# Last channel stage of an inverse 2D FFT: even classes as pairs of 64 by 64 products, joined on VectorE

## Chip, core and metric

The kernel runs on one core of a Trainium2 chip. The metric is device microseconds (us) of one execution of the kernel, as a median over runs. Engines are written as in the profile: PE is TensorE (matmuls), PEld its weight loads, DVE is VectorE, ACT is ScalarE, POOL is GpSimd, SP is SyncE, which issues most DMAs here.

## What is computed

Two branches work on the same layer norm of x (2048 tokens by 512 channels, bfloat16) and are added to x:

```
xn = _layernorm(A_x)
X  = rfft2(xn, axes=(-2, -1)) * (w_r + 1j*w_i)          # tokens and channels
A  = irfft2(X, s=(2048, 512), axes=(-2, -1))
B  = (gelu(xn @ w_gate) * (xn @ w_up)) @ w_down         # 512 -> 1792 -> 512
out = A_x + A + B
```

## The kernel before

All operations are put down in a list, each with an engine, an assumed cost, what it reads and writes, and a key. A planner (`_Sched`) simulates them and fixes one static order for each engine; a semaphore count joins engines. PE gets the spectral products as soon as the plan has their inputs ready, and the dense products of branch B as filler in all other places.

Branch B works on four blocks of 512 tokens and 14 slices of 128 hidden columns. `gated` (L718) makes four 128x512 products for gate and four for up into one of three PSUM banks each, ACT evicts them (L723 gelu into `gg`, L724 copy into `uu`, four buffers each), and DVE multiplies (L725) into `hT`. `down` (L766) sums 14 products into the bank `ps_dn`; ACT evicts it (L774 into `db`, two buffers) and DVE adds it to `x_sb` (L775). For the last block, `down` goes to `ps_sp` and DVE adds straight from PSUM (L777); these are the last 70 matmuls of the program.

Branch A is a DFT in stages. Forward over channels (L635), DVE butterflies, forward over tokens (L850, and L854 for class v=0), the filter on DVE, then the two stages that matter here:

- **Inverse token products, `f_i`.** Eight classes v; in each, for two halves kp and for even and odd channel frequencies o, one product with the real part (L931) and one with the imaginary part (L932). The spectrum X is the stationary operand, 128 channel frequencies taken with step 2, so that output partition (lane) = channel frequency. Each is a 128x128 product that streams 128 columns: eight to a class, 64 in all. ACT evicts each class from a pair of PSUM banks (L937).
- **Last channel stage, `f_b`.** After butterflies over tokens (DVE, through the helper `tt`, L467), DVE makes `zi` in `specC`. For each of eight pairs jp of token groups, eight products (L991) of 128 lanes by 128 columns: two token groups o by four classes cc (cosine even, cosine odd, sine even, sine odd frequencies; matrix `Ti`, 128 lanes x 128 positions each). ACT evicts 1024 columns (L996) into R in `specB`. DVE then adds and subtracts even and odd, cosine and sine, each time filling a mirrored half: `eo` (L467, 1024 elements, two), `y` (two), and adds `y` to `x_sb` (2048 elements). This goes on for each quarter jq, and SP stores the quarter of the output (L782).

The PSUM pairs of branch A come from a pool of two (`ps_sp`, name "sp" in the code). R, `eo` and `y` lie in `specB` (12288 elements a partition), which the token butterflies used before.

The products of the stage before the change, as the code has them:

```
for o in range(2):
    for cc in range(4):
        ins = e.matmul(spb(t, o, cc * P, P), zi.ap[:, 2 * jp + o, cc, :], Ti.ap[:, cc, :], start=(cc == 0), stop=(cc == 3))
```

One more place in the kernel matters for reading the change: L854, the v=0 class of the forward token stage. It multiplies 64 lanes by 512 columns, four times, the two halves of the lanes alternating and going to different PSUM banks:

```
for i in range(0 if v else 2):
    for r in range(2):
        l = slice(64 * r, 64 * r + 64)
        ins = e.matmul(spb(t, r), tf.ap[l, 2 * r + i], H.ap[l, hh[i]], start=(i == 0), stop=(i == 1))
```

Of the kernel before, what the change touches and what calls it, by code (L numbers as in the profile page):

```python
# [7 lines left out]
ACT = mybir.ActivationFunctionType  # L8
ALU = mybir.AluOpType
BF16 = mybir.dt.bfloat16  # L10
# [5 lines left out]
P = 128  # L16
# [21 lines left out]
def _constants():  # L38
    npbf = mybir.dt.np(BF16)
    th = 2.0 * np.pi / S  # L40
    m = np.arange(P)
    K = np.zeros((8, P))
    mm = 31 - m + 64 * (m // 32)
    K[0] = np.where(m < 64, 8 + 16 * mm, 16 * (mm - 63) * (m != 96))
    for c in range(1, 8):
        K[c] = c + 16 * mm
    q = np.arange(P) + 0.5
    ph = th * q[:, None, None] * K[None]
    co, si = np.cos(ph), np.sin(ph)
    si2 = si.copy()  # L50
    si2[:, 0, 96] = np.sin(th * q * 1024)
    cof = co.copy()
    cof[:, 0, 96] *= 0.5
    low = (m < 64)[None]
    tf = []
    for a in (cof, si2):
        for part in (1, np.where(low, -1, 1)):
            e = a[:64, 0] * part
            tf.append(np.concatenate([e, 0 * e] if a is cof else [0 * e, e]))
    for c in range(1, 8):  # L60
        r = np.sin(np.pi * c / 2)
        f = (r, r) if c % 2 else (-1.0, 1.0) if c == 4 else (1.0, -1.0)
        tf.append(np.concatenate([co[:64, c], f[0] * si[:64, c]]))
        tf.append(np.concatenate([co[:64, c], f[1] * si[:64, c]]))
    tf = np.stack(tf, 1)
    ci, sv = co[:64].transpose(2, 1, 0), si2[:64].transpose(2, 1, 0)
    sg = np.array([0, 1, 1, -1, 1, 1, 1, -1])[:, None]
    pr = np.concatenate([ci, -sg * sv], 2)
    pi = np.concatenate([sv, sg * ci], 2)
    lo = (m < 64)[:, None]  # L70
    for a in (pr, pi):
        half = a[:, 0, 0:64].copy()
        a[:, 0] = np.concatenate([half * ~lo, half * lo], 1)
    ti = np.stack([pr, pi, -pi], 2)
    a = 2.0 * np.pi / D * (np.arange(P) + 0.5)[:, None]
    ke = 2 * np.arange(P)[None]
    kse = ke.copy()
    kse[0, 0] = 256
    T = np.stack([np.cos(a * ke), np.cos(a * (ke + 1)), np.sin(a * kse), np.sin(a * (ke + 1))], 1)
    al = np.full((P, 4), 2.0)  # L80
    al[0, 0] = al[0, 2] = 1.0
    Ti = T.transpose(2, 1, 0) * al[:, :, None] / (S * D)
    fwd = []
    a = 2.0 * np.pi / D * (np.arange(P) + 0.5)[:, None]
    for r in (0, 2):
        kk = np.arange(r, 256, 4)[None]
        fwd += [np.cos(a * kk), np.sin(a * np.where(kk == 0, 256, kk))]
    odd = np.concatenate([np.arange(1, 256, 4), np.arange(3, 256, 4)])[None]
    fwd += [np.cos(a * odd), np.sin(a * odd)]
    small = np.concatenate([np.eye(P)] + fwd + [Ti.reshape(P, 512)], 1)  # L90

    def cvt(z):
        return np.ascontiguousarray(z.reshape(P, -1).astype(np.float32).astype(npbf))

    return cvt(small), cvt(tf), cvt(ti)
# [49 lines left out]
class _Sched:  # L145
# [11 lines left out]
    def op(self, eng, cost, fn, reads=(), writes=(), tiles=(), key=0.0, after=(), dma=0, lag=0.0, due=None, land=None):  # L157
        o = _Op()
        o.eng, o.fn, o.cost, o.key, o.dma, o.lag, o.due, o.land = eng, fn, cost, key, dma, lag, due, land
        o.reads, o.writes, o.tiles = reads, writes, [(t, False) for t in tiles]  # L160
        o.extra = [a for a in after if a is not None]
        o.seq = len(self.ops)
        o.end = None
        o.pos = None
        self.ops.append(o)
        return o
# [184 lines left out]
def bass_parallel_sum__spectral_gfnet__glu_gated_geglu__prompt_kernel(  # L351
# [22 lines left out]
    op = sch.op  # L374

    with ExitStack() as es:
        def sb(name, shape, dt=BF16, cell=0):
            n = int(np.prod(shape))
            t = es.enter_context(nc.sbuf_tensor(name, [P, n], dt))
            return view(t, name, 0, shape, cell)  # L380

        def view(t, name, lo, shape, cell=0):
            n = int(np.prod(shape))
            ap = t[:, lo:lo + n]
            if len(shape) > 1:
                names = "abcdef"[:len(shape)]
                ap = ap.rearrange("p (%s) -> p %s" % (" ".join(names), " ".join(names)), **dict(zip(names[1:], shape[1:])))
            return _V(ap, name, np.arange(lo, lo + n).reshape(shape), cell or (64 if n > 512 else 1))
# [8 lines left out]
        wu = sb("wu", [4, FF])  # L397
        wd = sb("wd", [NFC, D])
        small = sb("smallc", [9, P])
        tf = sb("tokf", [18, P])  # L400
        ti = sb("toki", [8, 3, P])
        W = sb("filt", [2, 2, 8, 257], cell=1)
        w1 = sb("filt1024", [2, 512])
        edge = sb("edge", [2, 8, 2])
# [10 lines left out]
        RB = region("specB", 12288)  # L415
# [7 lines left out]
        Ti = small[:, 5:9]  # L423
# [16 lines left out]
        def spb(t, h, lo=0, n=512):  # L440
            b = (2 * t.slot + h) * 512 + lo
            return ps_sp[:, b:b + n]

        def spair(t):
            return ps_sp[:, t.slot * 1024:(t.slot + 1) * 1024]
# [10 lines left out]
        def c_act(n):  # L456
            return 0.05 + n * 0.00085
# [8 lines left out]
        def tt(o, a, b, f, n, key=0.0, **kw):  # L466
            return op("dve", c_tt(n), lambda e: e.tensor_tensor(o.ap, a.ap, b.ap, f), reads=(a, b), writes=(o,), key=key, **kw)  # L467

        ADD, SUB, MUL = ALU.add, ALU.subtract, ALU.mult
# [114 lines left out]
        X = R1(0, [8, 2, D])  # L584
# [259 lines left out]
        for v, hh in ((4, (12, 13)), (0, (14, 15)), (2, (8, 9)), (6, (10, 11)), (1, (0, 1)), (7, (4, 6)), (3, (2, 7)), (5, (5, 3))):  # L844
            t = _T("sp")
# [73 lines left out]
        for i, v in enumerate((0, 4, 1, 7, 2, 6, 3, 5)):  # L919
            t = _T("sp")  # L920

            def f_i(e, v=v, t=t):
                ins = None
                xr, xi = ((0, 2), (1, 2)) if v == 0 else ((0, 3), (1, 1))
                for kp in range(2):
                    for o in range(2):
                        lo = 256 * kp + o
                        pr = X.ap[:, v, 0, lo:256 * kp + 256:2]
                        pi = X.ap[:, v, 1, lo:256 * kp + 256:2]
                        bank = spb(t, kp, 256 * o, 256).rearrange("p (x i) -> p x i", x=4)  # L930
                        e.matmul(bank[:, xr[0]:xr[0] + xr[1] + 1:xr[1]], pr, ti.ap[:, v, 0], start=(o == 0), stop=False)  # L931
                        ins = e.matmul(bank[:, xi[0]:xi[0] + xi[1] + 1:xi[1]], pi, ti.ap[:, v, 1 + kp], start=False, stop=(o == 1))  # L932
                return ins

            op("pe", 8 * 0.057, f_i, reads=(X[:, v], ti[:, v]), tiles=(t,), lag=0.1)
            gv = G[:, i].tr((1, 0, 2))
            op("act", c_act(1024), lambda e, gv=gv, t=t: e.activation(gv.ap, spair(t).rearrange("p (k x i) -> p k x i", k=4, x=4), ACT.Copy),  # L937
               writes=(gv,), tiles=(t,), key=-0.5)
# [36 lines left out]
            tt(Yb[:, h:h + 4], Yb[:, h:h + 4], od[:, h:h + 4], ADD, 2048)  # L975
        Yi = R1(0, [16, 2, 4, 64])
        zi = R3(0, [16, 4, P])
        R = RB(0, [8, 2, 4, P])
        for jq in range(4):
            js = slice(2 * jq, 2 * jq + 2)  # L980
            a = Yi[:, 4 * jq:4 * jq + 4]
            tt(zi[:, 4 * jq:4 * jq + 4, :, 64:P], a[:, :, 0], a[:, :, 1], ADD, 1024)
            tt(zi[:, 4 * jq:4 * jq + 4, :, 63::-1], a[:, :, 0], a[:, :, 1], SUB, 1024)
            for jp in (2 * jq, 2 * jq + 1):
                t = _T("sp")

                def f_b(e, jp=jp, t=t):
                    ins = None
                    for o in range(2):
                        for cc in range(4):  # L990
                            ins = e.matmul(spb(t, o, cc * P, P), zi.ap[:, 2 * jp + o, cc, :], Ti.ap[:, cc, :], start=(cc == 0), stop=(cc == 3))  # L991
                    return ins

                op("pe", 8 * 0.0565, f_b, reads=(zi[:, 2 * jp:2 * jp + 2], Ti), tiles=(t,), lag=0.1)
                rv = R[:, jp].rs([1024])
                op("act", c_act(1024), lambda e, rv=rv, t=t: e.activation(rv.ap, spair(t), ACT.Copy), writes=(rv,), tiles=(t,), key=-0.5)  # L996
            rf = R[:, js].rs([4, 4, P])
            eo = RB(8192, [4, 2, 256])
            y = RB(10240, [4, 512])
            tt(eo[:, :, :, 0:P], rf[:, :, 0::3], rf[:, :, 1:3], ADD, 1024)  # L1000
            tt(eo[:, :, :, 255:127:-1], rf[:, :, 0::3], rf[:, :, 1:3], SUB, 1024)
            tt(y[:, :, 0:256], eo[:, :, 0], eo[:, :, 1], ADD, 1024)
            tt(y[:, :, 511:255:-1], eo[:, :, 0], eo[:, :, 1], SUB, 1024)
            xc = x[:, 4 * jq:4 * jq + 4].rs([2048])
            tt(xc, y.rs([2048]), xc, ADD, 2048)
            if jq < 3:
                store(4 * jq, 4)
# [35 lines left out]
```

## Time and profile before

| what | value |
|---|---|
| time, median of 3 runs | 171.48 us (171.44 to 171.91) |
| the profiled execution, time | 171.29 us |
| the profiled execution, span | 169.4 us |
| PE busy | 166.3 us (98%), 999 matmuls |
| PEld busy | 86.1 us |
| DVE busy | 146.0 us (86%), 293 instructions |
| ACT busy | 106.3 us (63%) |
| granted PE clock | 1.0 in the whole span |
| `f_i`: L931 and L932 | 64 matmuls of 128x128, from 96.7 to 110.4 us |
| `f_b`: L991 | 64 matmuls of 128x128, from 129.3 to 138.6 us |

The span is the time from the first to the last instruction; 1.9 us of the execution lie outside it. A matmul's duration in the groups is its latency (219 ns for 128 columns); matmuls overlap, so what one takes on PE is read from the chain of work or from start to start.

### The profile page before, as it was taken

How to read it: one execution, taken by the hardware profiler on the slowest of the kernel's cores; microseconds unless marked ns; L12 is line 12 of the kernel's file. 1: busy time of each engine (PE TensorE's matmuls, PEld its weight loads, DVE VectorE, ACT ScalarE, POOL GpSimd, SP SyncE). 2: the span in 40 equal slices, each digit the busy share in tenths (PEclk: the TensorE clock that was granted, in tenths of full speed). 3: DMA queues.
4: the chain of work that ended last, by engine and by line, in shares of the span. 5: the costliest groups of instructions: out<-in, count | busy, mean ns of one | idle time of the engine just before them, and what ended most of it. 6: DMA issues, size and time to landing. Idle time of an engine off the chain costs nothing.

```text
span 169.4 us, 2695 instructions
## 1 busy us (share of the span) xinstructions
PE 166.3 (98%) x999; PEld 86.1 (51%) x999; DVE 146.0 (86%) x293; ACT 106.3 (63%) x174; POOL 12.3 (7%) x25
## 2 busy tenths in 40 slices
PE   8999999999999999999999999999999999999994
PEld 3698544445555444444444554644445654444443
DVE  2889999995975999999999999999999869963932
ACT  3588766663979739589663695875738896561000
POOL 2032253500000000020000000000000000000000
PEclk9999999999999999999999999999999999999999
DMA  5999999994025262510000000000000003300322
GB/s 146 338 350 347 286 132 300 224 255 101 0 55 127 76 136 79 159 61 0 0 0 0 0 4 0 0 0 0 4 0 2 0 4 106 128 13 0 124 67 62
DMA packets 22239, 15.62 MB, mean 92 GB/s; under 512 B 9293, under 2 KB 21586, under 8 KB 22226
## 3 DMA queue, kind: packets, MB, share of 16 engines
q1 hardware_dynamic: 21026, 14.63, 34.6%
q10 hardware_dynamic: 1200, 0.82, 1.6%
q8 instruction: 8, 0.13, 0.3%
q14 instruction: 5, 0.04, 0.1%
HBM read 11.38 MB, written 2.10 MB: 80 GB/s over the span
## 4 chain that ended last, share of the span: by engine, by line
PE 98%; DVE 0%; issue 0%
PE ps_gu L718 56%; PE ps_dn L766 21%; PE ps_sp L766 7%; PE ps_dn L476 3%; PE ps_sp L991 2%; PE ps_sp L635 2%; PE ps_sp L850 2%; PE ps_gu L737 1%; PE ps_sp L931 1%; PE ps_sp L932 1%; PE ps_dn L737 1%; PE ps_sp L550 1%; PE ps_sp L854 0%; DVE xnT L575 0%; DVE x_sb L777 0%; PE ps_sp L567 0%
## 5 line engine op out<-in xcount | busy, mean ns | idle before, releaser
L718 PE MATMUL ps_gu<-xnT,wg 128*128 128x512 bf16 (+1 forms) x236 | 56.7, 363 | 0.0
L718 PE MATMUL ps_gu<-xnT,wu 128*128 128x512 bf16 (+1 forms) x236 | 56.7, 363 | 0.0
L723 ACT ACTIVATE gg<-ps_gu 128x512 bf16<-128x512 f32 (+1 forms) x59 | 33.7, 572 | 12.2 <-PE ps_gu L718 8.9
L724 ACT ACTIVATE uu<-ps_gu 128x512 bf16<-128x512 f32 (+1 forms) x59 | 33.9, 575 | 10.5 <-PE ps_gu L718 10.2
L766 PE MATMUL ps_dn<-wd,hT 128*128 128x512 bf16 x168 | 38.9, 379 | 0.0
L467 DVE TENSOR_TENSOR specB<-specB 128x512 bf16<-128x512 bf16 (+2 forms) x58 | 33.6, 611 | 1.9 <-ACT specB L996 1.4
L718 PEld LDWEIGHTS ps_gu<-xnT,wu 128*128 128x128 bf16 x236 | 22.8, 98 | 23.1
L718 PEld LDWEIGHTS ps_gu<-xnT,wg 128*128 128x128 bf16 x236 | 22.6, 98 | 22.0 <-ACT uu L724 0.4
L766 PEld LDWEIGHTS ps_dn<-wd,hT 128*128 128x128 bf16 x168 | 16.3, 98 | 19.1
L725 DVE TENSOR_TENSOR hT<-gg,uu 128x512 bf16<-128x512 bf16 (+1 forms) x59 | 23.1, 395 | 1.8 <-ACT uu L724 1.8
L774 ACT ACTIVATE db<-ps_dn 128x512 bf16<-128x512 f32 x12 | 7.2, 597 | 18.4 <-PE ps_dn L766 18.4
L520 DVE BATCH_NORM_STATS2 bst<-x_sb 128x6 f32<-128x512 bf16 x16 | 10.9, 688 | 3.2 <-DMA x_sb<-in_A_x_dram 3.1
L467 DVE TENSOR_TENSOR specC<-specB 128x1024 bf16<-128x1024 bf16 (+2 forms) x18 | 12.4, 713 | 0.2
L766 PE MATMUL ps_sp<-wd,hT 128*128 128x512 bf16 (+2 forms) x70 | 12.3, 336 | 0.0
L467 DVE TENSOR_TENSOR specB<-specA 128x2048 bf16<-128x2048 bf16 x8 | 9.4, 1219 | 2.7 <-ACT specA L640 2.7
L775 DVE TENSOR_TENSOR x_sb<-db,x_sb 128x512 bf16<-128x512 bf16 x12 | 5.0, 420 | 5.4 <-ACT db L774 5.4
L467 DVE TENSOR_TENSOR specB<-specB,filt 128x2048 bf16<-128x2048 bf16 x8 | 9.4, 1221 | 0.0
L766 PEld LDWEIGHTS ps_sp<-wd,hT 128*128 128x128 bf16 x70 | 6.3, 98 | 6.1 <-DVE x_sb L777 0.2
L859 ACT ACTIVATE specA<-ps_sp 128x1024 bf16<-128x1024 f32 x8 | 7.8, 1035 | 1.3 <-PE ps_sp L850 1.3
L640 ACT ACTIVATE specA<-ps_sp 128x1024 bf16<-128x1024 f32 x8 | 7.7, 1023 | 1.2 <-PE ps_sp L635 1.2
L996 ACT ACTIVATE specB<-ps_sp 128x1024 bf16<-128x1024 f32 x8 | 7.8, 1031 | 0.8 <-PE ps_sp L991 0.8
L937 ACT ACTIVATE specC<-ps_sp 128x1024 bf16<-128x1024 f32 x8 | 7.8, 1039 | 0.0
(71 smaller groups left out, 130.0 us busy)
## 6 DMA issues: line engine op xcount, KB each, us to landing
out_dram<-x_sb SPq DMA_DIRECT2D x15, 128.0 KB, 1.8
wd<-in_B_w_down_dram SPq DMA_DIRECT2D x1, 1792.0 KB, 8.6
x_sb<-in_A_x_dram SPq DMA_DIRECT2D x3, 512.0 KB, 9.2
wg<-in_B_w_gate_dram SPq DMA_DIRECT2D x2, 512.0 KB, 8.6
wu<-in_B_w_up_dram SPq DMA_DIRECT2D x2, 512.0 KB, 9.2
toki<-c_ti SPq DMA_DIRECT2D x1, 768.0 KB, 4.4
tokf<-c_tf SPq DMA_DIRECT2D x1, 576.0 KB, 4.8
x_sb<-in_A_x_dram SPq DMA_DIRECT2D x4, 128.0 KB, 3.5
```

The source lines that it names most:

```text
L467: return op("dve", c_tt(n), lambda e: e.tensor_tensor(o.ap, a.ap, b.ap, f), reads=(a, b), writes=(o,), key=key, **kw)
L520: op("dve", 0.61, lambda e: e.bn_stats(bst[:, s].ap, xs(s).ap), reads=(xs(s),), writes=(bst[:, s],), key=key, due=due, after=after)
L640: op("act", c_act(1024), lambda e, yv=yv, t=t: e.activation(yv.ap, spair(t).rearrange("p (s r i) -> p s i r", s=4, r=4), ACT.Copy), writes ...
L718: ins = e.matmul(gub(t, n), w.ap[:, dc, fc * P:(fc + 1) * P], xnT.ap[:, b, sl, dc, :], start=(dc == 0), stop=(dc == 3))
L723: op("act", c_act(n), lambda e: e.activation(gg.ap[:, gs.slot, 0:n], gub(g, n), ACT.Gelu_apprx_tanh), tiles=(g, gs), key=0.0)
L724: op("act", c_act(n), lambda e: e.activation(uu.ap[:, us.slot, 0:n], gub(u, n), ACT.Copy), tiles=(u, us), key=0.0)
L725: op("dve", c_tt(n), lambda e: e.tensor_tensor(hT.ap[:, h.slot, lo:lo + n], gg.ap[:, gs.slot, 0:n], uu.ap[:, us.slot, 0:n], MUL), tiles=(g ...
L766: ins = e.matmul(bank(), hT.ap[:, hs[(b, fc)].slot, sl * P:(sl + 1) * P], wd.ap[:, fc, lo:lo + n], start=(fc == 0), stop=(fc == NFC - 1))
L774: op("act", c_act(n), lambda e: e.activation(db.ap[:, d.slot, 0:n], bank(), ACT.Copy), tiles=(t, d), key=0.0)
L859: op("act", c_act(1024), lambda e, xv=xv, t=t: e.activation(xv.ap, spair(t), ACT.Copy), writes=(xv,), tiles=(t,), key=-0.5)
L937: op("act", c_act(1024), lambda e, gv=gv, t=t: e.activation(gv.ap, spair(t).rearrange("p (k x i) -> p k x i", k=4, x=4), ACT.Copy), writes ...
L996: op("act", c_act(1024), lambda e, rv=rv, t=t: e.activation(rv.ap, spair(t), ACT.Copy), writes=(rv,), tiles=(t,), key=-0.5)
```

## The change

Only the cosine-even and sine-even classes of the last channel stage are made otherwise. Their matrices have a symmetry: between position n and position 127-n, a lane's value stays or changes its sign by the parity of the lane. So it is enough to multiply lanes of each parity by 64 positions; the sum of both products is one half of the result and the difference, mirrored, the other.

- `_constants`: the rows of the two even matrices `Ti` are sorted by parity (64 and 64).
- `f_i`: to have the lanes of the even channel frequencies sorted in the same way, each of the 32 products for o = 0 is made as two of 64 output lanes (stationary operand 128x64, step 4). They still stream 128 columns. Both write the same PSUM bank, in different halves of the partitions. The o = 0 products of a class now come first (eight), then the four whole ones for o = 1.
- `f_b`: four 128x128 products for the odd classes, and then eight of 64 lanes by 64 columns for the even ones, the two halves of the lanes alternating and going to different banks.
- DVE: for each jp one sum and one difference of 256 elements, 16 in all, on what ACT has evicted.
- R grows to all of `specB` (six slots of 128 for each token group); `eo` and `y` move into the buffers of `toki` and `tokf`, whose matrices have been read by then.

```diff
+    for i in (0, 2):
+        Ti[:, i] = np.concatenate([Ti[i // 2::2, i], Ti[1 - i // 2::2, i]])
...
-                for kp in range(2):
-                    for o in range(2):
+                for o in range(2):
+                    for kp in range(2):
                         lo = 256 * kp + o
-                        pr = X.ap[:, v, 0, lo:256 * kp + 256:2]
-                        pi = X.ap[:, v, 1, lo:256 * kp + 256:2]
                         bank = spb(t, kp, 256 * o, 256).rearrange("p (x i) -> p x i", x=4)
-                        e.matmul(bank[:, xr[0]:xr[0] + xr[1] + 1:xr[1]], pr, ti.ap[:, v, 0], start=(o == 0), stop=False)
-                        ins = e.matmul(bank[:, xi[0]:xi[0] + xi[1] + 1:xi[1]], pi, ti.ap[:, v, 1 + kp], start=False, stop=(o == 1))
+                        for ri, xx in ((0, xr), (1, xi)):
+                            xx = slice(xx[0], xx[0] + xx[1] + 1, xx[1])
+                            to = ti.ap[:, v, ri * (1 + kp)]
+                            for h in range(2) if o == 0 else ():
+                                l = slice(64 * (h ^ kp), 64 * (h ^ kp) + 64)
+                                ins = e.matmul(bank[l, xx], X.ap[:, v, ri, lo + 2 * h:256 * kp + 256:4], to, start=(ri == 0), stop=False)
+                            if o:
+                                ins = e.matmul(bank[:, xx], X.ap[:, v, ri, lo:256 * kp + 256:2], to, start=False, stop=(ri == 1))
...
-        R = RB(0, [8, 2, 4, P])
+        R = RB(0, [16, 6, P])
+        eo = view(ti_t, "toki", 0, [4, 2, 256])
+        y = view(tf_t, "tokf", 0, [4, 512])
...
                     for o in range(2):
-                        for cc in range(4):
-                            ins = e.matmul(spb(t, o, cc * P, P), zi.ap[:, 2 * jp + o, cc, :], Ti.ap[:, cc, :], start=(cc == 0), stop=(cc == 3))
+                        for i in range(2):
+                            ins = e.matmul(spb(t, o, i * P, P), zi.ap[:, 2 * jp + o, 2 * i + 1, :], Ti.ap[:, 2 * i + 1, :], start=(i == 0), stop=False)
+                    for o in range(2):
+                        for i in range(2):
+                            for h in range(2):
+                                l = slice(64 * h, 64 * h + 64)
+                                ins = e.matmul(spb(t, h, 256 + 128 * o + 64 * i, 64), zi.ap[l, 2 * jp + o, 2 * i, :], Ti.ap[l, 2 * i, 0:64], start=False, stop=(o + i == 2))
...
-                op("pe", 8 * 0.0565, f_b, reads=(zi[:, 2 * jp:2 * jp + 2], Ti), tiles=(t,), lag=0.1)
+                op("pe", 6 * 0.0565, f_b, reads=(zi[:, 2 * jp:2 * jp + 2], Ti), tiles=(t,), lag=0.1)
...
+            for j in range(4 * jq, 4 * jq + 4, 2):
+                ra, rb = (R[:, j + h, 2:4].rs([2, 2, 64]) for h in range(2))
+                tt(R[:, j:j + 2, 4:6, 0:64], ra, rb, ADD, 256)
+                tt(R[:, j:j + 2, 4:6, 127:63:-1], ra, rb, SUB, 256)
+            tt(eo[:, :, :, 0:P], rf[:, :, 4:0:-3], rf[:, :, 0:6:5], ADD, 1024)
+            tt(eo[:, :, :, 255:127:-1], rf[:, :, 4:0:-3], rf[:, :, 0:6:5], SUB, 1024)
```

The instructions of both programs, engine by engine: PE, DVE and ACT keep their order but for the stages named, and these: the last two `f_b` now stand side by side on PE (between them stood one group of four L718), and one group of four L718 and one of seven L766 behind them change places. SP issues the same DMAs in the same order.

More of the change, by code (lines that the diff above doesn't have):

```diff
@@ L399, in bass_parallel_sum__spectral_gfnet__glu_gated_geglu__prompt_kernel @@
         small = sb("smallc", [9, P])
-        tf = sb("tokf", [18, P])
-        ti = sb("toki", [8, 3, P])
+        tf_t = es.enter_context(nc.sbuf_tensor("tokf", [P, 18 * P], BF16))
+        ti_t = es.enter_context(nc.sbuf_tensor("toki", [P, 24 * P], BF16))
+        tf = view(tf_t, "tokf", 0, [18, P])
+        ti = view(ti_t, "toki", 0, [8, 3, P])
         W = sb("filt", [2, 2, 8, 257], cell=1)
@@ L977, in bass_parallel_sum__spectral_gfnet__glu_gated_geglu__prompt_kernel @@
         zi = R3(0, [16, 4, P])
-        R = RB(0, [8, 2, 4, P])
+        R = RB(0, [16, 6, P])
+        eo = view(ti_t, "toki", 0, [4, 2, 256])
+        y = view(tf_t, "tokf", 0, [4, 512])
         for jq in range(4):
-            js = slice(2 * jq, 2 * jq + 2)
             a = Yi[:, 4 * jq:4 * jq + 4]
@@ L989, in f_b @@
                     for o in range(2):
-                        for cc in range(4):
-                            ins = e.matmul(spb(t, o, cc * P, P), zi.ap[:, 2 * jp + o, cc, :], Ti.ap[:, cc, :], start=(cc == 0), stop=(cc == 3))
-                    return ins
-                op("pe", 8 * 0.0565, f_b, reads=(zi[:, 2 * jp:2 * jp + 2], Ti), tiles=(t,), lag=0.1)
[L995 to L1001, printed above, removed]
+                        for i in range(2):
[5 more added lines that the diff above has]
+                                ins = e.matmul(spb(t, h, 256 + 128 * o + 64 * i, 64), zi.ap[l, 2 * jp + o, 2 * i, :], Ti.ap[l, 2 * i, 0:64], start=False, stop=(o + i == 2))
+                    return ins
+                op("pe", 6 * 0.0565, f_b, reads=(zi[:, 2 * jp:2 * jp + 2], Ti), tiles=(t,), lag=0.1)
+                rv = R[:, 2 * jp:2 * jp + 2, 0:4]
+                op("act", c_act(1024), lambda e, rv=rv, t=t: e.activation(rv.ap, spair(t).rearrange("p (a c b) -> p a c b", a=2, c=4), ACT.Copy), writes=(rv,), tiles=(t,), key=-0.5)
+            rf = R[:, 4 * jq:4 * jq + 4]
+            for j in range(4 * jq, 4 * jq + 4, 2):
[4 more added lines that the diff above has]
+            tt(eo[:, :, :, 255:127:-1], rf[:, :, 4:0:-3], rf[:, :, 0:6:5], SUB, 1024)
             tt(y[:, :, 0:256], eo[:, :, 0], eo[:, :, 1], ADD, 1024)
```

## The prediction, made before the changed kernel ran

> **What bounds the kernel.** I read the page first (busy shares, slices, chain), then the chain of work in order of time, then DVE's timeline around the last stage. From the page:
>
> ```profile
> PE 166.3 (98%) x999; PEld 86.1 (51%) x999; DVE 146.0 (86%) x293; ACT 106.3 (63%) x174; POOL 12.3 (7%) x25
> ...
> PE   8999999999999999999999999999999999999994
> ...
> PEclk9999999999999999999999999999999999999999
> ...
> PE 98%; DVE 0%; issue 0%
> ```
>
> PE is busy in every slice at full granted clock, and the chain that ends last is PE work for 98% of the span. So the time is a sum over PE instructions: whatever PE takes longer or shorter in the two changed stages moves the end by as much, as long as nobody else makes PE wait. The chain in order of time gives the prices (start, us, what):
>
> ```profile
> 53.50 5.18 PE ps_gu L718 x24
> ...
> 61.70 1.73 PE ps_gu L718 x8
> 63.42 0.43 PE ps_sp L850 x2
> 63.86 0.54 PE ps_sp L854 x4
> 64.39 5.29 PE ps_gu L718 x24
> ...
> 129.41 0.89 PE ps_sp L991 x16
> ...
> 155.02 12.14 PE ps_sp L766 x70
> 167.18 0.29 DVE x_sb L777
> ```
>
> Three prices. (1) A 512-column product takes 5.18 / 24 = 0.216 us. (2) A 128x128 product takes 0.89 / 16 = 0.0556 us; a line through both is 0.0022 us + 0.000417 us a column, so 64 columns alone would be 0.029 us. (3) L854 is the only place with products of half the array: four of 64 lanes by 512 columns in 0.54 us, where four whole ones would take 0.86. So two halves do run together (two slots, 0.432 us), but 0.54 - 0.43 = 0.11 us is left over. And the 24 L718 products straight behind it took 5.29 instead of 5.18, another 0.11 us. I read that as the price of going from whole-array to half-array products and back: 0.22 us a round trip.
>
> **The change, part by part.** The sum is made against the profiled execution: 171.29 us, of which 169.4 span and 1.9 outside; the median of the runs is 0.19 above it.
>
> *Round trips.* Each `f_i` now makes its o = 0 products in half-array form and ends with four whole ones; each `f_b` starts with four whole ones and ends with eight in half-array form, and whole ones follow. Neighbouring `f_i` or `f_b` do not share a visit, because each has both kinds inside. So 8 + 8 = 16 round trips. At 0.22 us: **+3.5 us**. Bounds: 0 (if the two 0.11 are something else) and 0.22.
>
> *`f_b`, the even classes.* Before, four slots of 0.0556 for each jp; after, four pairs of 64-column products. A pair costs between 0.029 (the line above, halves together as in L854) and 0.0556 (no gain over 128 columns); four more matmuls and loads to a jp come with it. I take 0.035, near the lower end, because L854's two halves cost little more than one: 8 x 4 x (0.0556 - 0.035) = **-0.66 us**; bounds 0 and -0.85. The Trainium skill ("TensorE: Matmul & The Clock Gate", Wait — 56ns, not 53.3ns?) says that starts of matmuls are never under about 25 ns apart; a pair would then be 50 ns and the saving only 8 x 4 x 5.6 ns = 0.18 us, which would put the time 0.5 us higher. The trace speaks against that for halves: the four weight loads of L854 together took 0.11 us at 0.094 each, and its four products fit in two 512-column slots.
>
> *`f_i`, o = 0.* Before, four slots to a class; after, four pairs of 128 columns with 64 output lanes. If the two run together a pair takes what one took: **0 us**. If they do not, each class takes four slots more: 8 x 4 x 0.0556 = +1.8 us. No product with 64 output lanes is in the trace; the nearest row is L854 (64 input lanes), where halves run together, so I take 0 and keep 1.8 for the range. Nothing is saved here in any case: the columns streamed are the same.
>
> *DVE.* 16 additions of 256 elements. A 512-element one holds DVE for 0.33 us (two in 0.75, the last of 0.42) and L725's 256-element form is 274 ns against 417, so 0.33 - 0.14 = 0.19 to 0.20 us each: +3.2 us on DVE. They cost nothing if DVE has that much idle time between its first evicted R and the last thing PE needs from it. DVE's timeline (start, us, what, in brackets the idle time before):
>
> ```profile
> 135.75 0.42 DVE L775 TENSOR_TENSOR x_sb<-db,x_sb 128x512 bf16<-128x512 bf16 x1 [0.66 <-ACT db L774]
> 137.58 2.62 DVE L467 TENSOR_TENSOR specB<-specB 128x1024 bf16<-128x1024 bf16 x4 [1.41 <-ACT specB L996]
> ...
> 150.94 0.43 DVE L725 TENSOR_TENSOR hT<-gg,uu 128x512 bf16<-128x512 bf16 x1 [0.31 <-ACT uu L724]
> 152.67 0.43 DVE L725 TENSOR_TENSOR hT<-gg,uu 128x512 bf16<-128x512 bf16 x1 [1.30 <-ACT uu L724]
> 155.69 0.42 DVE L775 TENSOR_TENSOR x_sb<-db,x_sb 128x512 bf16<-128x512 bf16 x1 [2.60 <-ACT db L774]
> ...
> 160.00 0.69 DVE L777 TENSOR_TENSOR x_sb<-ps_sp,x_sb 128x512 bf16<-128x512 f32 x1
> ```
>
> The idle pieces are 0.66 + 1.41 + 0.31 + 1.30 + 2.60 = 6.3 us, and every one waits for PE through ACT, so they grow when PE is late. The new additions wait for ACT's evictions of R; queued behind them on DVE are the L725 products, whose `gg` and `uu` buffers (four each) ACT needs before PE gets a bank back: four gated pairs at 1.73 us give 6.9 us of room. The DVE steps from 155.69 on keep their order and stay tied to PE's last `ps_dn`. So I put DVE at **0**; with that cover gone, at most the 3.2 us themselves.
>
> *The rest.* ACT's eviction of R writes the same 1024 elements with gaps (1031 ns a piece before): 0. `eo` and `y` in other buffers: the matrices there were last read in `f_i`, some 20 us earlier, so no wait: 0. Two `f_b` side by side need both PSUM pairs, and the second waits for an ACT eviction that has 1.73 us of L718 ahead of it: 0. SP issues the same DMAs: 0.
>
> **Sum:** +3.5 - 0.66 + 0 + 0 = +2.85 us. 171.29 + 2.85 = 174.14 for an execution like the profiled one, 174.3 against the median.
>
> **The rivals.**
>
> *A, no price for going back and forth (faster).* The trace has a single round trip, in 512-column products, and at both edges PE's load also stood behind a semaphore (the load of the L718 behind L854 is 0.42 us idle, put down to ACT's `uu`). If the 0.11s were these waits, all that is left is the saving in `f_b`: 171.48 - 0.66 = 170.8 us (170.6 at best). It decides where a round trip costs less than 0.66 / 16 = 0.041 us. Against it: that `uu` was evicted by 64.06 (63.46 + 0.60), 0.26 us before the load that started at 64.32; the other edge is marked "issue", with nothing to wait for; and two unrelated waits would hardly be 0.11 both. Chance 0.10.
>
> *B, only the 64-lane form of `f_b` has the price.* `f_i`'s 64-column weights are another kind of half; if going to them and back is free, eight round trips are left: +1.75 - 0.66 = +1.1, 172.6 us. For it: no row shows it. Against it: nothing in the trace tells the two kinds apart. The Trainium skill ("TensorEngine Tiling (Array Packing)", Key Properties) says that any change of the tiling mode drains TensorE; by that rule the time is the forecast's, and no run so far shows it for columns. Chance 0.12.
>
> *C, the two 64-lane products of `f_i` do not overlap.* Each takes its own slot: 1.8 us more, 174.3 + 1.8 = 176.1 us. For it: no row shows overlap of output halves, and both write one PSUM bank, which L854's halves do not. The Trainium skill ("TensorEngine Tiling (Array Packing)", Restrictions) says that column tiling turns off Fast Weight Load, and "TensorE: Matmul & The Clock Gate", LDWEIGHTS, puts a plain load at 1/1.2 ns a column; my estimate from these pages is 53 ns for 64 columns, 107 for a pair one after the other, 1.6 us more in all. Chance 0.22.
>
> *D, DVE holds PE up.* Forecast plus up to 3.2 us; I count 0.5 to 2, 174.8 to 176.3. Against it stand the 6.3 us above. Chance 0.04.
>
> That the products do not come out as said is not a rival: the built program has them on PE as 64-lane pairs, and 128x64 by eights.
>
> **How the numbers follow.** Forecast 0.52, A 0.10, B 0.12, C 0.22, D 0.04. The forecast's own range is 174.1 to 175.0 (the pair cost of `f_b` at both ends). The range of 8 in 10 takes in B's and C's values with their neighbourhood: 172.4 to 176.4; A and tails are left out. About 0.3% (0.5 us) is what a measurement of this kernel can tell. Faster by over that: A at 0.09; within: 0.03, a mixture of small prices; slower: 0.88.
>
> **What would show it.** In the profile after: `f_b`'s two products of a pair starting together; L1000 and L1005 for one jp filling about 0.57 us of the chain (0.44 before), `f_i` about 0.67 (0.44 before); the piece behind each some 0.1 longer than its matmuls; PE still about 98% and the chain without DVE. It is wrong if the pieces of the chain fill only their slots (A), if `f_i` takes near 0.9 (C) or 0.44 (B), or if DVE's products L725 show no idle time before them and PE waits for ACT (D).

## The result and the profile after

The changed kernel takes **174.27 us** (median of 5 runs, 174.16 to 174.57) where the kernel before takes 171.48: 1.015 times as long, 95% interval 1.0118 to 1.0183. The profiled execution took 174.21 us with a span of 172.4; before it was 171.29 and 169.4. So the loss is 2.8 us by the medians and 3.0 us by the spans, and the 3.0 can be found in the chain of work.

From the page of the changed kernel, the line of busy times and the chain by engine:

```profile
PE 168.9 (98%) x1063; PEld 86.1 (50%) x1063; DVE 149.6 (87%) x309; ACT 107.0 (62%) x174; POOL 11.4 (7%) x25
...
PE 95%; DVE 2%; DMA 1%; ACT 1%; issue 0%
```

PE is as full as before and 2.6 us longer; DVE's 16 new instructions make it 3.6 us longer. The chain has a few percent of DVE, DMA and ACT in it now; they lie in the first 10 us, where the chain is followed back to the first rows of x by another way, and not at the changed stages. The chain in order of time at these (start, us, what), first one class of `f_i` before the change, then the changed kernel:

```profile
99.96 0.06 PE ps_sp L931
...
100.41 3.02 PE ps_dn L766 x14
```

```profile
107.99 0.39 PE ps_sp L938 x8
108.39 0.33 PE ps_sp L940 x4
...
131.59 0.22 PE ps_sp L1000 x4
131.82 0.22 PE ps_sp L1005 x8
132.04 0.33 PE ps_sp L1000 x4
132.37 0.22 PE ps_sp L1005 x8
132.59 0.97 PE ps_gu L722 x4
...
158.03 12.14 PE ps_sp L770 x70
```

A class of `f_i` is now 0.39 + 0.33 = 0.72 us; before, its eight products filled 100.41 - 99.96 = 0.45 us (8 x 0.0556 = 0.445). That is 0.275 us a class, 8 x 0.275 = 2.2 us. Two `f_b` are 0.22 + 0.22 + 0.33 + 0.22 = 0.99 us, and the four L722 behind them 0.97 instead of 0.86: 1.10 together, against 0.89 before. That is 4 x 0.21 = 0.84 us. The sum is 3.04 us, the whole loss. The last stage, 70 L770 in 12.14 us, has not changed; it starts at 158.03 instead of 155.02.

Four whole products behind halves fill 0.33, four in front of them 0.22: the return to the whole form is again 0.11 us, and in `f_i` (L938 to L940) it stands between instructions of one operation, with no semaphore between them.

The way in stands inside one operation too, in `f_b` (L1000 to L1005), and PE's weight loads show what is lost there (start, us, what; of the eight loads of L1005 the first two):

```profile
131.54 0.10 PEld L1000 LDWEIGHTS ps_sp<-smallc,specC 128*128 128x128 bf16 x1
131.75 0.10 PEld L1005 LDWEIGHTS ps_sp<-smallc,specC 64*128 64x128 bf16 x2
```

The loads of whole products follow each other every 0.056 us, each about 0.05 us ahead of its product. The load at 131.54 is that of the last whole product, which starts at 131.60. The first loads of halves come only 0.20 us later, and their products start with them: the weights of the new form are not loaded ahead, as those of the same form are. At the way in of `f_i` it is the same (a load at 108.44, the first of the halves at 108.64).

### The profile page after: what moved, and what is told of

Same layout as the page of the kernel before. It is cut to its first block, busy times and chain, and to the rows that moved or that the text cites. A ratio compares the mean times of both kernels' runs of the same rounds, so it can differ in the third digit from the quotient of the medians.

```text
span 172.4 us, 2839 instructions
## 1 busy us (share of the span) xinstructions
PE 168.9 (98%) x1063; PEld 86.1 (50%) x1063; DVE 149.6 (87%) x309; ACT 107.0 (62%) x174; POOL 11.4 (7%) x25
## 4 chain that ended last, share of the span: by engine, by line
PE 95%; DVE 2%; DMA 1%; ACT 1%; issue 0%
PE ps_gu L722 55%; PE ps_dn L770 21%; PE ps_sp L770 7%; PE ps_sp L639 2%; PE ps_sp L938 2%; PE ps_sp L854 2%; PE ps_sp L940 2%; DMA x_sb<-in_A_x_dram 1%; PE ps_sp L1000 1%; PE ps_sp L1005 1%; PE ps_gu L741 1%; DVE bst L524 1%; ACT gg L755 1%; PE ps_sp L554 0%; PE ps_sp L858 0%; PE ps_dn L741 0%
## 5 line engine op out<-in xcount | busy, mean ns | idle before, releaser
L722 PE MATMUL ps_gu<-xnT,wu 128*128 128x512 bf16 (+1 forms) x236 | 56.7, 363 | 0.1
L722 PE MATMUL ps_gu<-xnT,wg 128*128 128x512 bf16 (+1 forms) x236 | 56.8, 363 | 0.0
L770 PE MATMUL ps_dn<-wd,hT 128*128 128x512 bf16 x168 | 38.9, 379 | 0.0
L722 PEld LDWEIGHTS ps_gu<-xnT,wu 128*128 128x128 bf16 x236 | 22.8, 98 | 23.7 <-ACT gg L755 0.4
L722 PEld LDWEIGHTS ps_gu<-xnT,wg 128*128 128x128 bf16 x236 | 22.5, 98 | 22.1 <-ACT uu L728 0.4
L471 DVE TENSOR_TENSOR specB<-specB 128x512 bf16<-128x512 bf16 (+3 forms) x58 | 27.1, 500 | 1.8 <-ACT specB L1010 1.3
L770 PEld LDWEIGHTS ps_dn<-wd,hT 128*128 128x128 bf16 x168 | 16.3, 98 | 19.2
L770 PE MATMUL ps_sp<-wd,hT 128*128 128x512 bf16 (+2 forms) x70 | 12.3, 336 | 0.0
L770 PEld LDWEIGHTS ps_sp<-wd,hT 128*128 128x128 bf16 x70 | 6.3, 98 | 6.1 <-DVE x_sb L781 0.2
L1010 ACT ACTIVATE specB<-ps_sp 128x1024 bf16<-128x1024 f32 x8 | 7.9, 1025 | 1.4 <-PE ps_sp L1005 1.4
```

The source lines that it names most:

```text
L722: ins = e.matmul(gub(t, n), w.ap[:, dc, fc * P:(fc + 1) * P], xnT.ap[:, b, sl, dc, :], start=(dc == 0), stop=(dc == 3))
L770: ins = e.matmul(bank(), hT.ap[:, hs[(b, fc)].slot, sl * P:(sl + 1) * P], wd.ap[:, fc, lo:lo + n], start=(fc == 0), stop=(fc == NFC - 1))
```

## Experiments

Theory: PE's work sets the time, and each visit to the half form (going there and back) has a price of its own, whatever is done in it. Rivals: DVE's additions hold PE up; only one of the two stages pays; the price is by product and not by visit. The kernel before took 171.27 us beside the first four kernels and 171.36 beside the last two.

**One stage at a time.** First `f_i` alone (the stage behind it as before, the even matrices sorted):

```diff
 # kernel before, plus
+    for i in (0, 2):
+        Ti[:, i] = np.concatenate([Ti[i // 2::2, i], Ti[1 - i // 2::2, i]])
 # and f_i of the changed kernel
```

> Only the inverse token products are in 64-lane halves (with the rows of the two even matrices sorted to match); the last channel stage keeps its eight whole 128x128 products and DVE adds nothing. Theory (PE sum, every visit to the half form is paid): in the profile of the changed kernel a class of f_i fills 0.39 + 0.33 = 0.72 us of the chain against 0.44 before, so 8 x 0.28 = +2.2 us, 173.7 us. Rival B (only 64-lane inputs pay): no change, 171.5 us. Rival D (DVE's 16 additions are what delays): no change, 171.5 us.

Measured: 173.41 us, 2.1 over the kernel before (ratio 1.0117, 1.01 to 1.0134). Nothing was added on DVE here, and 64 output lanes pay as well as 64 input lanes. Rival B (only 64-lane inputs pay) falls.

Then the last stage alone:

```diff
 # changed kernel, with f_i of the kernel before
```

> Only the last channel stage is changed (64 by 64 products and the 16 additions on DVE); the inverse token products are whole as before, so the lanes of the even classes reach the stage unsorted and the output is not the reference's. Theory: a pair of f_b fills about 1.11 us of the chain against 0.89 before, 4 x 0.22 = +0.9 us, 172.35 us. Rival D (DVE): nearly all of the loss is here, 174 us. Rival A (no price for a visit): 170.8 us.

Measured: 172.05 us, 0.8 over the kernel before (ratio 1.0041, 1.0028 to 1.0053). Rival A (no price for a visit) would have made it faster. 2.1 + 0.8 is the loss of both together, to within 0.2 us (2.8 by the medians, 3.0 by the spans).

**DVE.**

```diff
-                tt(R[:, j:j + 2, 4:6, 0:64], ra, rb, ADD, 256)
-                tt(R[:, j:j + 2, 4:6, 127:63:-1], ra, rb, SUB, 256)
```

> The changed kernel without the 16 sums and differences on DVE; the slots that they fill are read with what lay there, so the output is not the reference's. Theory (DVE's 3.2 us lie in its idle time): no change, 174.3 us. Rival D (DVE holds PE up): faster by what it holds up, 0.5 to 2 us, 172.3 to 173.8 us.

Measured: 174.34 us, 0.07 us from the changed kernel; against the kernel before beside it the ratio is 1.0178 (1.0155 to 1.02), where the changed kernel had 1.015. The page of this run shows the work gone:

```profile
PE 168.0 (97%) x1050; PEld 86.0 (50%) x1063; DVE 146.1 (85%) x293; ACT 107.0 (62%) x174; POOL 11.4 (7%) x25
```

DVE is 146.1 us again instead of 149.6, and the time does not fall. So the 16 additions lie in time that DVE had to spare. DVE's timeline of the changed kernel shows two of them, and its idle time further on (start, us, what, the idle time before):

```profile
136.62 0.49 DVE L471 TENSOR_TENSOR specB<-specB 128x256 bf16<-128x256 bf16 x2 [0.42 <-ACT specB L1010]
...
155.67 0.42 DVE L729 TENSOR_TENSOR hT<-gg,uu 128x512 bf16<-128x512 bf16 x1 [0.87 <-ACT uu L728]
158.70 0.43 DVE L779 TENSOR_TENSOR x_sb<-db,x_sb 128x512 bf16<-128x512 bf16 x1 [2.60 <-ACT db L778]
```

DVE still sits idle 0.87 and 2.60 us there, waiting for ACT.

**By visit or by product.** The same instructions with the order turned in every second class, so that neighbours meet half to half (shown in part; the start and stop flags follow the order):

```diff
-                for o in range(2):
+                for o in (1, 0) if i % 2 == 0 else (0, 1):
...
+                    for part in (whole, halves) if jp % 2 == 0 else (halves, whole):
+                        ins = part()
```

> The changed kernel with the order inside every second f_i and f_b turned round, so that two neighbours share a visit to the half form: first class whole then halves, second halves then whole. Same instructions, same work. On PE the four pairs of f_b and two pairs of classes of f_i stand side by side, so six of 16 visits go. Theory: 4 x 0.20 for f_b and 2 x 0.26 for f_i (there the first weights of a visit cost 0.05 more) = -1.3 us against the changed kernel, 172.9 us. Rival (the loss is per instruction, by the 64 more matmuls and loads, and not by visit): no change, 174.3 us.

Measured: 173.32 us (ratio 1.0113, 0.9 to 1.4% over the kernel before); the span of the profiled execution is 171.3, 1.1 us under the changed kernel's. The run without the additions, made beside it, took 174.16 to 175.22 us, and this one 172.92 to 173.76. The gain is a little less than expected, and the chain of this run shows why:

```profile
96.92 0.39 PE ps_sp L938 x8
97.30 0.55 PE ps_sp L940 x8
97.85 0.39 PE ps_sp L938 x8
...
108.21 0.63 PE ps_sp L938 x16
...
131.32 0.22 PE ps_sp L1001 x4
131.54 0.34 PE ps_sp L1009 x16
131.88 0.33 PE ps_sp L1001 x4
132.22 0.86 PE ps_gu L722 x4
```

At 96.92 PE took the second class ahead of the first, so they met whole to whole and no visit was saved. Five of 16 visits went, not six: 4 x 0.20 + 0.26 = 1.06 us, which is the 1.1 us by which the span is shorter. The lines also give the parts of a visit. In `f_b`, 16 halves in one visit take 0.34 us and eight 0.22: four more pairs cost 0.12, so a pair is 0.030 us and the way in 0.22 - 0.12 = 0.10. The way out is 0.11. A pair of `f_b` with one shared visit is 0.22 + 0.34 + 0.33 = 0.89 us, exactly what it was before the change. In `f_i`, 16 halves take 0.63 and eight 0.39: 0.060 a pair, and 0.15 for the way in.

**All products of `f_i` in halves** (the last stage as before), against the price by product; the lines show the difference to `f_i` of the changed kernel:

```diff
-                            if o:
-                                ins = e.matmul(bank[:, xx], X.ap[:, v, ri, lo:256 * kp + 256:2], to, start=False, stop=(ri == 1))
+                            for h in range(2) if o else ():
+                                l = slice(64 * h, 64 * h + 64)
+                                ins = e.matmul(bank[l, xx], X.ap[:, v, ri, lo + 128 * h:256 * kp + 128 * h + 128:2], to, start=False, stop=(ri == 1))
```

> As the kernel with f_i alone in halves, but the four whole products for o = 1 are made as 64-lane pairs too: 16 half products a class, nothing whole, so a class changes form only at its ends and two neighbouring classes share a visit (two pairs stand side by side on PE). Theory (the price is by visit): the two shared visits save 2 x 0.26 = 0.5 us, and 32 pairs at 0.060 in place of 32 whole products at 0.056 cost 0.14: 0.4 us less than with the even products alone in halves, so +1.7 us over the kernel before. Rival (the price is by half product): twice as many half products, twice the loss, +4.2 us over the kernel before.

Measured: 172.87 us, 1.5 over the kernel before (ratio 1.0085, 1.006 to 1.0109), where the even ones alone in halves cost 2.1. The two intervals touch, but a price by product would have made twice the loss, 4.2 us, of twice the half products. It falls.

**Why `f_i`'s visit costs more than `f_b`'s.** The kernel with `f_i` alone in halves again and the same number of halves, but of neighbouring lanes, so that the weights are read with step 2 (shown in part):

```diff
-lo + 2 * h:256 * kp + 256:4]
+lo + 128 * h:256 * kp + 128 * h + 128:2]
```

> As the kernel with f_i alone in halves, but each half takes 64 neighbouring lanes (stationary operand 128x64 with step 2 as before the change, instead of step 4), and the rows of the even matrices are unsorted again; the result is the same function. It asks why the first pair of a visit takes 0.106 us to the next one instead of 0.056, and later pairs 0.060. Theory 1 (loads of 64 columns are slow whatever the step): the weight loads still last 0.13 to 0.16 us each in the profile, a class still fills 0.72 us, 2.1 us over the kernel before. Theory 2 (step 4 makes the loads slow): loads fall to about 0.1 us and a class to 0.67 us or under, 1.7 us over the kernel before.

Measured: 173.12 us, 1.8 over the kernel before (ratio 1.0096, 1.0073 to 1.0119; step 4 had 1.0117). The two ratios overlap, but the profiles tell the runs apart. The groups of 64-column weight loads, first of the changed kernel and then of this run (busy us, mean ns of one):

```profile
L938 PEld LDWEIGHTS ps_sp<-toki,specA 128*64 128x64 bf16 x64 | 2.6, 145 | 2.8 <-ACT specC L945 0.8 <-issue 0.8 <-DVE specA L902 0.4
```

```profile
L934 PEld LDWEIGHTS ps_sp<-toki,specA 128*64 128x64 bf16 x64 | 2.0, 110 | 2.8 <-issue 1.3 <-ACT specC L941 0.8 <-DVE specB L467 0.4
```

A load of 64 columns takes 145 ns with step 4 and 110 with step 2 (whole loads of 128 columns, step 2: 98). In the chain of this run a class is:

```profile
107.90 0.35 PE ps_sp L934 x8
108.24 0.33 PE ps_sp L936 x4
```

That is 0.67 to 0.68 us instead of 0.72, so step 4 costs some 0.045 us a class, 0.3 to 0.4 us in all. Neither theory was right alone: step 4 makes the loads slower, and 64 columns with step 2 are still slower to load than 128. The first pair of a visit, whose weights are not loaded ahead, feels that: in the trace the second pair starts 0.106 us behind it with step 4 and 0.077 with step 2. Later pairs start 0.060 and 0.055 us apart. What is left, 0.675 - 0.445 = 0.23 us, is the price of the visit.

No version here beats the kernel before. With every `f_b` visit shared by two, which fills the two PSUM pairs, the last stage comes out even (0.89 against 0.89), and what `f_i` pays to sort its lanes is lost. By these numbers a gain would need two things, lanes sorted by other means than halves in `f_i` and three or more `f_b` to a visit; neither was tried.

## Why the prediction was right

The time was forecast at 174.3 us and is 174.27. That is closer than the terms were, because two of them missed on opposite sides; that they cancel is luck. The loss itself, 2.8 us by the medians and 3.0 by the spans, is no surer than 0.2 us either. One `f_b` fills 0.55 us with its way out (forecast 0.57), a class of `f_i` 0.72 (forecast 0.67).

- **What bounds:** right. The loss is the sum of PE's work in two stages, and the chain shows no other engine there.
- **Round trips, +3.5 us:** right. The single visit in the trace before, 0.11 us each way with 512-column products, was a good price for others: 0.21 in `f_b`, 0.23 in `f_i` with step 2. Sixteen at 0.21 are 3.4 us. Turning the order to share visits gave back what this says.
- **`f_b`, -0.66 us:** right in mechanism, a little small. A pair is 0.030 us (forecast 0.035), so 32 x (0.0556 - 0.030) = -0.82 us. The floor of about 25 ns between starts that the Trainium skill gives ("TensorE: Matmul & The Clock Gate", Wait — 56ns, not 53.3ns?) would have made a pair 50 ns; the trace does not agree. The two products of a pair start 3 to 4 ns apart there, and 16 products in a visit take 0.34 us, 21 ns each with the way in counted; only products of the same half keep 0.030 us between them.
- **`f_i`, 0 us:** the two halves of a pair do overlap, as taken. But the term left out that their weights load more slowly: 0.05 us more on the way in and 0.060 instead of 0.056 for a pair, 8 x 0.065 = +0.5 us. This is the term that was mis-sized. It was hedged as rival C (1.8 us more, pairs one after the other), which did not come; the Trainium skill's sentence that column tiling turns off Fast Weight Load ("TensorEngine Tiling (Array Packing)", Restrictions) fits with the 110 ns against 98, but no run here shows that this is the reason. The pairs' loads go side by side (eight of 145 ns fill 0.33 us on PEld), so my estimate of 107 ns a pair was far off.
- **DVE, 0 us:** right in effect (0.07 us without the additions). Where two follow each other they take 0.49 us, and one alone has 285 ns, so each holds DVE for 0.20 us as forecast; that busy time grew by 3.6 and not 3.2 us fits with the tails of those that nothing follows at once.
- **The rest:** two `f_b` side by side made no wait, and the moves of `eo` and `y` and the strided eviction show none (L1010 takes 1025 ns; before 1031).
- **Rivals:** A falls by the way in from L1000 to L1005 and the way back from L938 to L940, 0.10 and 0.11 us with no semaphore between; B by `f_i` alone; C by the pairs of `f_i`, 0.060 us each and not 0.111; D by the run without the additions. The rule that any change of tiling mode drains TensorE (the Trainium skill, "TensorEngine Tiling (Array Packing)", Key Properties) fits with the first loads of halves, which come 0.20 us behind the load before, for rows (131.54 to 131.75) and for columns (108.44 to 108.64).

## What to carry to other kernels

Splitting a product for half the array pays only if the streaming that it saves in one visit is more than 0.21 us, here some eight products of 128 columns made as pairs of 64 (0.026 us saved on each); count visits, not products, and order the work so that half products of neighbours meet. When a change pays for a saving on one stage by preparing its input on another, price the preparation first: here it cost 2.2 us, and the 0.82 us that the last stage streams less was itself outweighed by that stage's own visits (8 x 0.21 = 1.7 us). One odd line in a trace (four products in 0.54 us, and the next group 0.11 too long) was enough to price the largest term of the change.

## What the runs showed of the hardware

- Going from whole-array products to halves costs 0.10 to 0.11 us for 64 input lanes (`f_b` with 64 columns, L854 with 512) and, with the slower first pair, 0.12 (step 2) to 0.15 (step 4) for 64 output lanes (`f_i`, 128 columns). Coming back costs 0.11 in all of them.
- On the way from whole products of 128 columns to halves, the first weight load comes 0.20 us behind the last one of the old form, where the loads of these whole products follow each other every 0.056 us.
- Half products run two at a time in either direction, also when both write the same PSUM bank in different partitions (`f_i`).
- A weight load of 64 columns, made in pairs, takes longer than one of 128 (110 ns against 98, both at step 2), and the step of its columns in SBUF matters: 145 ns at step 4. The prediction had not counted this.
- In one visit, 16 products of 64 by 64 took 0.34 us with 0.10 for the way in, 15 ns for each product.
